# Sparse attention and a mixture of experts: row sends with mask products between them, and a routing without pieces on the shared port

## The chip, the cores and the metric

The kernel runs on one core of one Trainium2 chip. The time is the device time of one execution in microseconds (us). Three runs of the kernel before took 984.45, 992.74 and 991.97 us, a median of 991.97 us. The execution that the profiler recorded took 990.66 us; its span, from the first to the last recorded instruction, is 988.6 us.

The engines are TensorE (PE, with its weight loads as PEld), VectorE (DVE), ScalarE (ACT), GpSimd (POOL) and SyncE (SP, which issues DMAs). Each runs its own instructions in a fixed order.

## The reference

Two layers follow each other. The first is attention for 4 batches of 8 heads, 576 positions, 64 values per head, in which each query keeps only its 32 largest scores. The second is a layer of 8 experts over the 2304 rows of 512 values that attention gives; each row goes to the two experts with the largest noisy logits.

```python
scores = scale * np.matmul(q, k.transpose(0, 1, 3, 2))
kth = np.partition(scores, -top_k, axis=-1)[..., -top_k:-top_k + 1]   # top_k = 32
scores = np.where(scores >= kth, scores, -1000000000.0)
attn = np.exp(scores - max) / sum;  out = np.matmul(attn, v)
...
noisy_logits = x @ w_gate + np.log1p(np.exp(x @ w_noise)) * noise
top2_w = softmax of the two largest noisy logits of a row
h = np.maximum(x[mask] @ w1[e], 0.0)                                  # 512 -> 1024
out[mask] += top2_w[mask, k, None] * (h @ w2[e])                      # 1024 -> 512
```

## The kernel before

**Attention.** A tile is 128 queries of one head against its 576 keys; 36 tiles make a batch, 144 all four. For a tile PE computes the scores into two PSUM banks (L602, L606), ScalarE copies the first half to SBUF (L614), VectorE folds the halves to their maxima and minima (L636) and finds the 32nd largest value by rounds of "eight largest" (L649) and "replace these eight" (L654). In some tiles (the table `DROPS`, in tenths of a batch's tiles) one replacement is done by ScalarE and GpSimd instead: a sign (L660) and a product (L663). A small piece makes the exponential's bias (L670, on GpSimd or VectorE). A mask of what is below the 32nd value is made by ScalarE (L717, with its threshold from L713) or by VectorE (L679). The **mask product** (L727, nearly always on GpSimd) puts the mask on the scores, ScalarE takes the exponential (L675), PE transposes the tile (L750, L754), ScalarE copies it (L759, L763), and PE multiplies it with the values (L812 to L824). Rows are scaled by their sums (L870 to L882) and collected in `xr`. From batch 1 on keys and queries are split into a high and a low part (L537, L541, L544).

**Routing.** After a batch's 36 tiles its logits are ready. `route` computes the noise scale, the two largest logits, the gates and the slot of each row in its expert's list with small pieces on ScalarE, VectorE and GpSimd (L985 to L1062). Then GpSimd issues ten **row sends**, indirect DMAs that write each row of `xr` into its two experts' lists in DRAM (`scatter`, L1111, with a small memset before each, L1110). They are issued in a chain in which a send waits only until the one ahead has begun.

**Experts.** The lists are worked off in five groups: rows 0 to 127 of all 8 experts after batch 0, rows 128 to 255 of experts 4 to 7 after batch 1, and after batch 2 rows 256 to 383 of experts 4 to 7 and rows 128 to 383 of experts 0 to 3; the last group, 256 rows of all experts, comes after batch 3. SP loads the rows (L1205), PE transposes them (L1236) and multiplies. One-tile groups use plain float32 (L1301, L1328). The two groups with two tiles split each weight into a high half (ScalarE, L1182) and a low half (L1186, on GpSimd or VectorE) and take three products per pair (L1270 to L1272 up, L1336 to L1338 down). A **unit** is one such up and down step for 128 of an expert's 1024 hidden values; a group of four experts has 32 units, the last one 64. Results go out by indirect DMAs on GpSimd (L1356).

**The order.** All pieces are given to a planner (`Plan`, L93) with an engine, a planned duration, what they need, and a priority; it plays the engines' clocks forward and writes down the order in which each engine then runs its instructions. A piece with an `alt` can go to a second engine, and tables by batch (`BIAS`, `BELOW`, `NORM`, `OUTS`, `LOWS`) weigh the choice. `PACE` and `WHEN` set priorities of expert work, transposes and routing against attention. Until the first expert rows are there PE's idle times are filled with matmuls on a dummy tile (`filler`, L564). The planned durations are not times of the chip; they only move the order. The sends of batch b are added like this:

```python
scat.append(add("POOL", 1280, scatter(t, k), [x, g, AVN["tok", b]] + [(s, True) for s in scat[-1:]] + FILLS,
                move=750, lat=700))
```

## Time and profile before

| | |
|---|---|
| median of three runs | 991.97 us (984.45 to 992.74) |
| profiled execution | 990.66 us, span 988.6 us |
| PE busy | 926.3 us, 94% |
| VectorE busy | 683.0 us, 69% |
| ScalarE busy | 651.5 us, 66% |
| GpSimd busy | 650.5 us, 66% |
| row sends (L1111) | 40, 40.9 us |
| mask products on GpSimd (L727) | 141, 187.4 us |
| low weight halves on GpSimd (L1186) | 79, 194.6 us |

Busy time is an average over parts of the span with different limits, so it is read by stretches. A busy PE is not PE at its peak, since matmuls overlap and their ends are modelled. In the timeline an idle time stands in brackets with what ended it. A line such as L727 is the line of the kernel above.

### The profile page before, as it was taken

The page shows a single profiled execution, that of the slowest core. Times are in us where ns is not written, and L with a number is a line of the kernel's source. Part 1 is how long each engine was busy: PE and PEld are TensorE (multiplying, and loading weights), DVE is VectorE, ACT ScalarE, POOL GpSimd, SP SyncE. Part 2 cuts the span into 40 slices and gives each one's busy share as a digit, 9 for nine tenths or more (in the row PEclk, how much of TensorE's full clock was granted, in tenths as well). Part 3 has the DMA queues.
Part 4 walks back from the last instruction along what each step waited for, and adds up shares of the span by engine and source line. Part 5 has one row for each costly group of instructions (what it writes and reads, how often), then busy time and mean ns, then how long its engine had stood idle before and what let it go on. Part 6 is the DMA issues. An engine that isn't in the chain of part 4 may idle for free.

```text
span 988.6 us, 18573 instructions
## 1 busy us (share of the span) xinstructions
PE 926.3 (94%) x6229; PEld 711.0 (72%) x6246; DVE 683.0 (69%) x2191; ACT 651.5 (66%) x1502; POOL 650.5 (66%) x819
## 2 busy tenths in 40 slices
PE   9999999799999778999989999999898999999993
PEld 4555566477778567777767777778787999998992
DVE  7999989989999969999979992347644222222220
ACT  4888887388988467988737873356644555555550
POOL 4566576646755856566676662238878898888881
PEclk9999999999999989999999999999999999999997
DMA  9464521346687566665856787785658687777741
GB/s 288 161 208 151 174 71 45 110 124 192 189 235 190 209 194 175 189 204 185 227 190 207 229 264 244 260 266 202 171 160 272 213 253 224 226 228 235 214 107 25
DMA packets 122250, 190.61 MB, mean 193 GB/s; under 512 B 8224, under 2 KB 69664, under 8 KB 122144
## 3 DMA queue, kind: packets, MB, share of 16 engines
q1 hardware_dynamic: 113440, 169.10, 54.0%
q0 software_dynamic: 8704, 20.22, 9.4%
q8 instruction: 51, 0.84, 0.3%
q14 instruction: 55, 0.45, 0.2%
HBM read 153.02 MB, written 36.27 MB: 191 GB/s over the span
## 4 chain that ended last, share of the span: by engine, by line
PE 59%; DVE 17%; ACT 8%; POOL 6%; issue 4%; DMA 2%; another core or an unknown queue 1%; SPq 0%; POOLq 0%; DVEq 0%; ACTq 0%
PE hps L1301 6%; DVE t8s L649 6%; PE bk L1328 6%; PE bk L602 5%; DVE cat L654 4%; PE hps L564 4%; PE hps L1270 4%; PE hps L1272 4%; PE hps L1271 4%; PE pp L750 4%; PE bank L812 3%; DVE cat L636 3%; PE bk L606 3%; PE bk L1336 2%; PE bk L1337 2%
## 5 line engine op out<-in xcount | busy, mean ns | idle before, releaser
L649 DVE MAX8 t8s<-cat 128x8 f32<-128x288 f32 (+3 forms) x576 | 265.3, 489 | 4.7 <-POOL cat L663 2.4
L727 POOL TENSOR_TENSOR ss<-ss,mk 128x576 f32<-128x576 f32 x141 | 187.4, 1331 | 76.5 <-ACT mk L717 57.2
L1186 POOL TENSOR_TENSOR wl<-wr,wh 128x1024 fp32r<-128x1024 f32 x79 | 194.6, 2529 | 35.8 <-ACT wh L1182 29.5
L654 DVE MATCH_REPLACE8 cat<-t8s,cat 128x208 f32<-128x208 f32 (+2 forms) x415 | 162.7, 394 | 0.0
L636 DVE TENSOR_TENSOR cat<-bk,ss 128x288 f32<-128x288 f32 x288 | 126.3, 443 | 34.7 <-ACT ss L614 28.3
L675 ACT ACTIVATE ss<-ss,nb 128x576 f32<-128x576 f32 x144 | 112.6, 782 | 39.9 <-POOL ss L727 37.1
L614 ACT ACTIVATE ss<-bk 128x288 f32<-128x288 f32 x288 | 111.5, 416 | 39.6 <-PE bk L606 15.1
L1328 PE MATMUL bk<-wr,hh 128*128 128x512 f32 x256 | 127.8, 595 | 0.0
L1301 PE MATMUL hps<-xh,wr 128*128 128x128 f32 x1024 | 127.5, 279 | 0.0
L1301 PEld LDWEIGHTS hps<-xh,wr 128*128 128x128 f32 x1024 | 123.1, 195 | 5.2 <-issue 4.0
L1182 ACT ACTIVATE wh<-wr 128x1024 fp32r<-128x1024 f32 x96 | 99.8, 1055 | 34.8 <-PE bk L1338 17.1
L1280 DVE SCALAR_TENSOR_TENSOR hl<-hps,hh 128x256 fp32r<-128x256 f32 x96 | 40.3, 422 | 111.2 <-ACT hh L1276 109.5
L1270 PE MATMUL hps<-xh,wh 128*128 128x256 f32 x384 | 111.3, 290 | 0.2
L606 PE MATMUL bk<-hi 128*128 128x288 f32 x240 | 88.9, 380 | 24.1 <-ACT ss L614 12.6
L1272 PE MATMUL hps<-xh,wl 128*128 128x256 f32 x384 | 108.8, 283 | 0.4 <-POOL wl L1186 0.4
L1271 PE MATMUL hps<-xl,wh 128*128 128x256 f32 x384 | 108.6, 283 | 0.0
L717 ACT ACTIVATE mk<-ss,under 128x576 bf16<-128x576 f32 x118 | 91.2, 778 | 19.8 <-POOL under L713 11.2
L759 ACT ACTIVATE pt<-pp 128x512 f32<-128x512 f32 x144 | 86.8, 603 | 15.3 <-PE pp L750 14.3
L750 PE MATMUL pp<-ident,ss 128*128 128x128 f32 x576 | 90.2, 279 | 6.4 <-ACT pt L759 3.6
L750 PEld LDWEIGHTS pp<-ident,ss 128*128 128x128 f32 x576 | 66.4, 142 | 40.4 <-ACT pt L759 11.9
L1356 POOL DMA_INDIRECT out_dram<-yo,tok x40 | 65.1, 1627 | 38.1 <-ACT yo L1352 29.8
L564 PE MATMUL hps<-dummy 128*128 128x512 bf16 x283 | 80.0, 395 | 2.4 <-DVE dummy L458 0.9
(159 smaller groups left out, 1910.5 us busy)
## 6 DMA issues: line engine op xcount, KB each, us to landing
wr<-in_w_dram SPq DMA_DIRECT2D x224, 512.0 KB
raw<-in_qk_dram SPq DMA_DIRECT2D x48, 320.0 KB
xg<-xs SPq DMA_DIRECT2D x16, 528.0 KB
xs<-xg SPq DMA_DIRECT2D x12, 528.0 KB
vt<-in_v_dram SPq DMA_DIRECT2D x32, 192.0 KB
out_dram<-xs SPq DMA_DIRECT2D x1, 5120.0 KB
xs<-xg SPq DMA_DIRECT2D x16, 264.0 KB
hi<-in_qk_dram SPq DMA_DIRECT2D x8, 320.0 KB
```

The source lines that it names most:

```text
L564: nc.tensor.matmul(ps, C["dummy"].to_broadcast([128, 128]), C["dummy"].to_broadcast([128, 512]), start=True, stop=True)
L636: nc.vector.tensor_tensor(o, t["sp", 1], t["s"][:, :HS], op=op)
L649: return lambda: nc.vector.max(t["t8"][:, r], t["cat"] if r == 3 else t["cat"][:, slice(*TAKE[r])])
L654: nc.vector.match_replace(g, t["t8"][:, r], g, NEG)
L727: ENG[eng].tensor_tensor(t["s"], t["s"], t["mk"], op=OP.subtract)
L750: nc.tensor.transpose(pp[:, c], t["s"][:, k0 + c * 128:k0 + (c + 1) * 128], ident)
L1186: return lambda eng: ENG[eng].tensor_tensor(WS[m][1][:, i], W[m][:, i], WS[m][0][:, i].bitcast(F32), op=OP.subtract)
L1270: nc.tensor.matmul(ps[:, :NN], ah, xh, start=(c == 0), stop=False)
L1271: nc.tensor.matmul(ps[:, :NN], ah, xl, start=False, stop=False)
L1272: nc.tensor.matmul(ps[:, :NN], al, xh, start=False, stop=(c == 3))
L1301: nc.tensor.matmul(ps[:, f * 128:(f + 1) * 128], w[:, 0, a:a + 128], X["h", e][:, c, :128], start=(c == 0), stop=(c == 3))
L1328: nc.tensor.matmul(Y[e][0], HN["h", ff // 2][:, f * 128:(f + 1) * 128], W[4 * e + ff // 2][:, 1, f * 512:(f + 1) * 512], start=(ff == 0), ...
```

## The change

Sends get a `gap`: the planner does not start a send before 1500 or 1600 of its nanoseconds have passed since its end of the one ahead (`SGAP`; `SLOT` 1 means every send), and other pieces take the time. In the routing GpSimd makes ex + 1 once (`one_more`) for its own error term and for VectorE's reciprocal, where VectorE made it a second time with a tensor_scalar; the marker column of `odd` is made by a scalar_tensor_tensor with a constant tile `away`. Planned durations of routing, value products, sums and output sends, and the tables of choices and priorities, are set anew.

```diff
-BIAS = (500, 500, 500, 500)
-BELOW = (1100, -3300, 2200, 4100)
+BIAS = (2000, 500, 500, 500)
+BELOW = (1100, -3100, 2200, 4500)
...
-LOWN = 16
+LOWN = 13
...
-DROPS = (4, 0, 1, 0)
+DROPS = (4, 0, 2, 0)
...
-WHEN = (16, 13, -21, -20)
+SGAP, SLOT = (1500, 1600, 1600, 1500), (1, 1, 1, 1)
+
+WHEN = (16, 13, -21, -12)
...
-PACE = [(70, 54), (900, 40), (90, 13), (300, 13), (0, 0)]
+PACE = [(70, 54), (910, 40), (110, 23), (300, 18), (0, 0)]
...
+            if x.gap:
+
+                at = self.sent + x.gap
+                if at > t:
+                    heapq.heappush(wait[e], (at, x.n, x))
+                    continue
...
+            if x.gap is not None:
+                self.sent = t + x.dur
...
         def err():
 
-            G.tensor_scalar(new("q", [NT, 8]), st["ex"], 1.0, None, op0=OP.add)
-            G.tensor_scalar(st["q"], st["q"], 1.0, None, op0=OP.subtract)
+            G.tensor_scalar(new("q", [NT, 8]), st["u"], 1.0, None, op0=OP.subtract)
             G.tensor_tensor(st["q"], st["q"], st["ex"], op=OP.subtract)
 
+        def one_more():
+            G.tensor_scalar(new("u", [NT, 8]), st["ex"], 1.0, None, op0=OP.add)
+
         def part():
-            V.tensor_scalar(new("u", [NT, 8]), st["ex"], 1.0, None, op0=OP.add)
-            V.reciprocal(st["u"], st["u"])
+            V.reciprocal(new("ru", [NT, 8]), st["u"])
...
-            V.tensor_scalar(new("tm", [2, NT, 9])[:, :, :, 8], st["c1"][:, None, :].to_broadcast([128, 2, NT]), 2.0, float(E * STRIDE),
-                            op0=OP.not_equal, op1=OP.mult)
+            V.scalar_tensor_tensor(new("tm", [2, NT, 9])[:, :, :, 8], st["c1"][:, None, :].to_broadcast([128, 2, NT]), 2.0,
+                                   C["away"][:, None, :].to_broadcast([128, 2, NT]), op0=OP.not_equal, op1=OP.mult)
...
-                                move=750, lat=700))
+                                move=750, lat=700, gap=(SGAP[b] if len(scat) % SLOT[b] == 0 else 0) if scat else 0))
```

The order on GpSimd where batch 1's rows are sent; L1110 and L1111 are a send with its memset. Before, from the end of the gates (L1030) on (six more sends follow, then the mask product L727):

```order
L1030 TENSOR_TENSOR xr<-p 128x5x8
L544 TENSOR_TENSOR hi<-raw,hi 64x640
L1110 MEMSET spacer 1x1
L1111 DMA xg<-xr,si 40960x528
L1110 MEMSET spacer 1x1
L1111 DMA xg<-xr,si 40960x528
L1110 MEMSET spacer 1x1
L1111 DMA xg<-xr,si 40960x528
L1110 MEMSET spacer 1x1
L1111 DMA xg<-xr,si 40960x528
```

After, where the mask product is L739, a send L1125, the bias L682 and an output send L1370:

```order
L1124 MEMSET spacer 1x1
L1125 DMA xg<-xr,si 40960x528
L725 TENSOR_SCALAR under<-t8s 128x1 x2
L739 TENSOR_TENSOR ss<-ss,mk 128x576
L1124 MEMSET spacer 1x1
L1125 DMA xg<-xr,si 40960x528
L739 TENSOR_TENSOR ss<-ss,mk 128x576
L725 TENSOR_SCALAR under<-t8s 128x1
L1369 MEMSET spacer 1x1
L1370 DMA out_dram<-yo,tok 2560x512
L1124 MEMSET spacer 1x1
L1125 DMA xg<-xr,si 40960x528
```

Between the first and the last send of a batch there are now 6, 8 and 6 mask products in batches 0, 1 and 2, where there was none. In batch 3, after attention, low weight halves (L1200) and output sends stand between them:

```order
L1043 TENSOR_TENSOR xr<-p 128x5x8
L1124 MEMSET spacer 1x1
L1125 DMA xg<-xr,si 40960x528
L1200 TENSOR_TENSOR wl<-wr,wh 128x1024
L1124 MEMSET spacer 1x1
L1125 DMA xg<-xr,si 40960x528
L1369 MEMSET spacer 1x1
L1370 DMA out_dram<-yo,tok 2560x512
L1124 MEMSET spacer 1x1
L1125 DMA xg<-xr,si 40960x528
```

On PE, the last tile's transposes (L750 before) stood among the units of the first two-tile group (L1270 to L1272 and L1336 to L1338); 14 of its 32 units were ahead of them:

```order
L1270 MATMUL hps<-xh,wh 128x256
L1271 MATMUL hps<-xl,wh 128x256
L1272 MATMUL hps<-xh,wl 128x256
L750 MATMUL pp<-ident,ss 128x128 x4
L754 MATMUL bank<-ident,ss 128x128
L1336 MATMUL bk<-wh,hh 128x512
L1337 MATMUL bk<-wl,hh 128x512
```

After, the same transposes (L762) stand among the last steps of the one-tile groups (L1315, L1342), and the first step of the first two-tile unit (L1284) follows:

```order
L1315 MATMUL hps<-xh,wr 128x128 x8
L1250 MATMUL hps<-ident,xs 128x128 x2
L762 MATMUL pp<-ident,ss 128x128 x4
L766 MATMUL bank<-ident,ss 128x128
L1250 MATMUL hps<-ident,xs 128x128 x2
L1342 MATMUL bk<-wr,hh 128x512
```

All 32 units now stand behind attention's last tile. At the front of PE's order 51 tiles' transposes stand ahead of the first expert transpose (45 before), with 314 filler matmuls (300 before). VectorE makes 19 of the 96 low halves (17 before), all after attention; 4 of batch 0's bias pieces (19 before); and 21 of the copies of L849 (27 before).

## Rows read from the trace of the kernel before

**Rows 1.** The page: busy time by engine; busy tenths in 40 slices.

```profile
PE 926.3 (94%) x6229; PEld 711.0 (72%) x6246; DVE 683.0 (69%) x2191; ACT 651.5 (66%) x1502; POOL 650.5 (66%) x819
...
PE   9999999799999778999989999999898999999993
...
DVE  7999989989999969999979992347644222222220
```

**Rows 2.** Windows: length, busy PE, PEld, DVE, ACT, POOL; clock, DMA share, GB/s.

```profile
180.00:200.00 20.00, 15.88 (x78) 9.22 (x77) 15.67 (x56) 7.43 (x17) 12.56 (x23) 0.91 0.36 123
...
340.00:360.00 20.00, 12.48 (x63) 9.21 (x62) 12.96 (x45) 6.82 (x18) 10.23 (x19) 0.83 0.51 175
500.00:520.00 20.00, 15.26 (x92) 11.39 (x89) 13.49 (x52) 6.64 (x16) 15.19 (x31) 0.93 0.64 211
...
600.00:728.00 128.00, 123.52 (x839) 99.42 (x838) 63.03 (x174) 67.23 (x153) 67.14 (x65) 1.00 0.69 220
```

**Rows 3.** Timeline of GpSimd: start, length, what, idle before; batches 0 and 1.

```profile
188.94 0.92 POOL L1111 DMA_INDIRECT xg<-xr,si  x1 [0.23 <-issue]
...
334.13 1.13 POOL L1111 DMA_INDIRECT xg<-xr,si  x1 [0.17 <-POOL spacer L1110]
...
346.06 0.92 POOL L1111 DMA_INDIRECT xg<-xr,si  x1 [0.24 <-issue]
347.04 1.27 POOL L727 TENSOR_TENSOR ss<-ss,mk 128x576 f32<-128x576 f32 x1
```

**Rows 4.** Timeline of VectorE, its idle times behind the sends of batches 0, 1, 2.

```profile
201.37 0.21 DVE L874 RECIPROCAL rs<-sums 128x9 f32<-128x9 f32 x1 [4.96 <-POOL sums L870]
...
350.51 0.46 DVE L636 TENSOR_TENSOR cat<-bk,ss 128x288 f32<-128x288 f32 x1 [2.58 <-ACT ss L614]
...
355.04 0.46 DVE L636 TENSOR_TENSOR cat<-bk,ss 128x288 f32<-128x288 f32 x1 [3.06 <-ACT ss L614]
...
365.98 0.22 DVE L874 RECIPROCAL rs<-sums 128x9 f32<-128x9 f32 x1 [2.25 <-POOL sums L870]
...
519.14 0.46 DVE L636 TENSOR_TENSOR cat<-bk,ss 128x288 f32<-128x288 f32 x1 [6.21 <-issue]
```

**Rows 5.** Timeline of PE: first expert matmul, a stall, last transposes, two units.

```profile
206.23 1.95 PE L1301 MATMUL hps<-xh,wr 128*128 128x128 f32 x16
...
350.23 0.61 PE L606 MATMUL bk<-hi 128*128 128x288 f32 x1 [7.52 <-ACT ss L614]
...
714.71 0.60 PE L750 MATMUL pp<-ident,ss 128*128 128x128 f32 x4
...
820.90 0.36 PE L1270 MATMUL hps<-xh,wh 128*128 128x256 f32 x1
...
823.95 0.36 PE L1270 MATMUL hps<-xh,wh 128*128 128x256 f32 x1
```

**Rows 6.** Waits of PE: us in total, times, longest.

```profile
PE hps L1272 <- POOL wl L1186: 0.4, 1, 0.4
```

**Rows 7.** Groups by line: count, busy us, mean ns, idle before.

```profile
L564 PE MATMUL hps<-dummy 128*128 128x512 bf16 x283 | 80.0, 395 | 2.4 <-DVE dummy L458 0.9 <-issue 0.9
...
L670 DVE TENSOR_SCALAR nb<-t8s 128x1 f32<-128x1 f32 x63 | 12.7, 202 | 0.6
...
L849 DVE COPY xr<-bank 128x256 f32<-128x256 f32 (+1 forms) x27 | 9.6, 355 | 26.9 <-PE bank L841 24.5 <-PE bank L754 0.9 <-ACT pt L925 0.9
```

**Rows 8.** Single lines: ns least, median, most; first and last start.

```profile
L999 DVE TENSOR_SCALAR u<-ex x4: 333/1116/1330, 163.1 to 728.2; 128x40 f32<-128x40 f32 x4
...
L1054 DVE TENSOR_SCALAR tm<-c x4: 1023/1406/2134, 170.0 to 735.7; 128x10 f32<-128x10 f32 x4
...
L1047 DVE TENSOR_TENSOR tm<-rank,oh x4: 244/274/1222, 174.7 to 738.2; 128x80 f32<-128x80 f32 x4
...
L1186 POOL TENSOR_TENSOR wl<-wr,wh x79: 2372/2415/3012, 660.2 to 960.9; 128x1024 fp32r<-128x1024 f32 x79
...
L1186 DVE TENSOR_TENSOR wl<-wr,wh x17: 1204/1224/2015, 663.1 to 950.6; 128x1024 fp32r<-128x1024 f32 x17
```

More of the change, by code (lines that the diff above doesn't have):

```diff
@@ L38 @@
 WEIGHS = (700, 2400, 2100, 3400)
-BIAS = (500, 500, 500, 500)
-BELOW = (1100, -3300, 2200, 4100)
+BIAS = (2000, 500, 500, 500)
+BELOW = (1100, -3100, 2200, 4500)
 LOWK = (2300, 1900, 500, 2600)
-OUTS = (300, 300, 300, 100)
-NORM = (3000, 400, -100, -200)
-LOWS = (2100, 1600, 2300)
-LOWN = 16
+OUTS = (300, -100, 300, 300)
+NORM = (3000, 400, -100, -1700)
+LOWS = (2100, 1600, 2700)
+LOWN = 13
 def spread(i, tenths):
@@ L84 @@
           (3, 384, 2, range(8))]
-PACE = [(70, 54), (900, 40), (90, 13), (300, 13), (0, 0)]
+PACE = [(70, 54), (910, 40), (110, 23), (300, 18), (0, 0)]
 class Node:
-    __slots__ = ("eng", "dur", "fn", "deps", "users", "prio", "left", "ready", "lat", "start", "n", "share", "move", "bank", "alt", "ready2", "shy", "lock")
+    __slots__ = ("eng", "dur", "fn", "deps", "users", "prio", "left", "ready", "lat", "start", "n", "share", "move", "bank", "alt", "ready2", "shy", "lock", "gap")
 class Plan:
@@ L105, in __init__, with add @@
         self.nodes, self.rings, self.prio, self.pauses = [], {}, 0, []
-    def add(self, eng, dur, fn, deps=(), prio=None, lat=0, share=1.0, move=0, bank=False, alt=None, lock=False):
+    def add(self, eng, dur, fn, deps=(), prio=None, lat=0, share=1.0, move=0, bank=False, alt=None, lock=False, gap=None):
         x = Node()
@@ L112, in add @@
         x.users, x.start, x.n, x.bank, x.alt = [], None, len(self.nodes), bank, alt
-        x.shy, x.lock = None, lock
+        x.shy, x.lock, x.gap = None, lock, gap
         self.nodes.append(x)
@@ L472, in sparse_attention_moe @@
     C["spacer"] = cp.tile([1, 1], F32, name="spacer")
+    C["away"] = cp.tile([128, NT], F32, name="away")
+    nc.vector.memset(C["away"], float(E * STRIDE))
     C["iota8"] = cp.tile([128, 8], F32, name="iota8")
@@ L825, in few @@
                                      stop=(c == 4), skip_group_check=True)
-        av = add("PE", 1200 if rest else 2350, few if rest else values, [x for m in pairs for x in PAIR[m]], share=0.5, bank=True)
+        av = add("PE", 735 if rest else 2315, few if rest else values, [x for m in pairs for x in PAIR[m]], share=0.5, bank=True)
         for m in pairs:
@@ L882, in norm @@
             ENG[eng].tensor_tensor(o, o, NN["r"][:64, 8:10, None].to_broadcast([64, 2, D]), op=OP.mult)
-        p1 = add("POOL", 170, plus, [T[i]["mid"][0] for i in range(j // 9 * 9, j // 9 * 9 + 9)])
-        r = add("DVE", 190, recip, [p1])
+        p1 = add("POOL", 345, plus, [T[i]["mid"][0] for i in range(j // 9 * 9, j // 9 * 9 + 9)])
+        r = add("DVE", 418, recip, [p1])
         br = pl.take("rs", 2, r)
@@ L1091, in route @@
         x1 = add("ACT", 220, ln, [x0])
-        x2 = add("POOL", 560, err, [x0])
-        pa = add("DVE", 330, part, [x0])
-        x2 = add("POOL", 760, noised, [x1, x2, pa, AVN["ax", b]])
+        x2 = add("POOL", 425, one_more, [x0])
+        pa = add("DVE", 325, part, [x2])
+        x2 = add("POOL", 765, err, [x2])
+        x2 = add("POOL", 1270, noised, [x1, x2, pa, AVN["ax", b]])
         x3 = add("DVE", 1200, top, [x2])
-        g = a2 = add("POOL", 320, apart2, [x3])
+        g = a2 = add("POOL", 440, apart2, [x3])
         g = add("ACT", 120, exp2, [g])
         g = add("DVE", 290, whole, [g])
-        g = add("POOL", 640, gates, [g, AVN["xr", b]])
+        g = add("POOL", 950, gates, [g, AVN["xr", b]])
         pm = add("PE", 880, mm, [x3], share=0.2, bank=True)
         pp = pl.take("ps_l", 1, pm)
-        od = add("DVE", 330, odd, [a2])
-        x = add("DVE", 690, slots, [pm, od, prev["cntn"] if prev else None], bank=True)
+        od = add("DVE", 340, odd, [a2])
+        x = add("DVE", 1000, slots, [pm, od, prev["cntn"] if prev else None], bank=True)
         pl.give(pp, x)
@@ L1363, in down @@
                     po = pl.take("yo", 2, y)
-                    z = add("POOL", 1280, st, [y], move=750, lat=700)
+                    z = add("POOL", 1850, st, [y], move=750, lat=700)
                     pl.give(po, z)
```

4 lines of the change are left out of this document (2 added, 2 removed).

## The prediction

> **What bounds the kernel now.** I read the page first. PE is busy for 94% of the span, no other engine for more than 69%, but the slices of the span show two halves: VectorE is at 9 tenths almost everywhere until the 24th slice (it ends at about 593 us) and then falls to 2 to 7 tenths and stays at 2 in the end, while PE stays at 9 [rows 1]. So attention runs at VectorE's pace where PE has little to do (batch 0: there are no expert rows yet and PE is kept going by filler matmuls), at the pace of both engines in batches 1 and 2, and at PE's pace from then on: between 600 and 728 us PE is busy for 123.5 of 128 us and VectorE for 63.0 [rows 2].
>
> The second look goes to the slices that break this pattern, 180 to 200, 340 to 360 and 500 to 520 us: PE drops to 15.9, 12.5 and 15.3 of 20 us, VectorE to 15.7, 13.0 and 13.5 [rows 2]. These are the places where GpSimd sends the rows of a batch. GpSimd's timeline shows batch 1's ten sends from 334.13 to 346.98 us, 1.3 us apart and with nothing but each send's own small memset between them; the first mask product stands behind the last one, at 347.04 [rows 3]. A mask product of 1.27 us feeds each tile's exponential, so for 13 us no tile can go on, and PE, ScalarE and VectorE run dry as their buffers fill.
>
> The third view, each engine's timeline behind the bursts, gives the size: VectorE stood idle for 4.96 us behind batch 0's sends, for 2.58, 3.06 and 2.25 behind batch 1's and for 6.21 behind batch 2's, 19.1 us in all [rows 4]; PE stood still for 7.52 us at once behind batch 1's [rows 5]. Batch 3's sends come after attention, where nothing but expert weights waits for GpSimd.
>
> **The change, part by part.** The times are set against the profiled execution, 990.66 us (span 988.6 us); the median of the three runs is 991.97, 1.3 us above it.
>
> *Sends apart.* The order after the change puts 6, 8 and 6 mask products between the first and the last send of batches 0, 1 and 2. Ten sends of 1.3 us and 6 to 8 products of 1.27 us [rows 3] make 20.5 to 23 us of GpSimd's time, with the small steps and key halves among them some 25 us, where 13 us stood before. In them 6 to 8 tiles move on, and none did. The gain is bounded by 0 (every stall comes back elsewhere) and 19.1 us (all of it goes). I take two thirds, **-12.7 us**: a product can still be late by one send (1.3 us), and the products wait in GpSimd's order for ScalarE's masks. What is late next is the last send, by about 12 us in each batch. In batch 0 the first expert matmul came 16.4 us after the last send's end (189.86, from 188.94 and 0.92 [rows 3]; 206.23 [rows 5]), so it comes later too; the order shows what PE does instead, 51 tiles' transposes ahead of the first expert transpose where 45 stood. That is attention work moved forward, not waiting. In batches 1 and 2 the rows sent are used only by the next groups, which stand 10 to 25 tiles later in PE's order.
>
> *Fillers.* PE's order holds 314 filler matmuls, 300 before. At 80.0 us for the 283 recorded [rows 7], 0.28 us each, 14 more are **+4.0 us** (0 if they only fill time in which PE would wait; I keep the 4).
>
> *Clock.* The granted clock was 0.91, 0.83 and 0.93 in the three slices [rows 2], against 1.00 from 600 to 728 us: 1.8, 3.4 and 1.4 us lost if PE had been busy throughout, 4.6 us at its busy shares of 0.79, 0.62 and 0.76. It was lowest in the slice where PE had stood still for 7.52 us. Part of that loss lies inside the stalls already counted, so I take **-2 us** (0 to -4.6).
>
> *Routing.* The +1 moves from VectorE to GpSimd (L999, median 1.12 us, least 0.33 [rows 8]), and the tensor_scalar of L1054 (median 1.41 us for ten columns [rows 8]) becomes a scalar_tensor_tensor that reads a second tile. The new form is not in the trace. Its nearest row is L1047, a two-tile operation of 80 columns: least 0.24, median 0.27, most 1.22 us [rows 8]. So each routing gives VectorE 1.3 to 2.3 us. A rule speaks against this edit: by the Trainium skill, SBUF — State Buffer, section "Who interferes with whom", a VectorE instruction with two inputs in SBUF still contends with a GpSimd instruction that reads SBUF, and whoever comes second is blocked for the whole of the other. By that rule the new form would often cost the 1.22 us and this edit would give the 1.3 us; the median of L1047 sides with 2.3 where GpSimd is not reading. GpSimd's own chain gets no shorter, since VectorE's reciprocal now waits for GpSimd's +1.
>
> *Constants.* They change only the order and who does a piece. In batch 0, 15 of the bias pieces go from VectorE to GpSimd (19 left it, now 4): 15 x 0.20 = 3.0 us of VectorE [rows 7]. GpSimd was 66% busy [rows 1] and hides them. Six copies of 0.36 us [rows 7] go from VectorE to ScalarE, four side drops more go to ScalarE and GpSimd. Batch 0, where VectorE alone sets the pace, gains 3.0 + 1.3 to 2.3 us, and I take 4.5; batches 1 and 2, where PE is as full as VectorE, gain 0 to 2.3 each and the copies 0 to 2.1, and I take 1.5: together **-6 us** (0 to -12).
>
> *The end of attention.* In PE's order 14 of the 32 units of the first two-tile group stood ahead of attention's last transposes; now none does. A unit is 3.05 us here (820.90 to 823.95 [rows 5]), so 43 us of expert work moves behind attention, and attention itself comes that much earlier; on a full PE this is a swap at no cost. Its cover is the supply of low weight halves. Around batch 3's sends GpSimd now has 4 halves, 10 sends and 3 output sends in one stretch, and VectorE makes more of the halves. PE waited 0.4 us for a half in the whole run [rows 6]. Between nothing and 20 us I take the end that this row is nearest to, **+2 us**.
>
> Sum: -12.7 + 4.0 - 2 - 6 + 2 = -14.7, so 990.66 - 14.7 = **976 us**.
>
> **The rivals.** *All of it comes back.* Every stall goes (-19.1), the clock stays up (-4.6), VectorE's pieces count in full (-12), and only the fillers are paid (+4): 959 us. For it: PE is the bound from 600 us on and idle nowhere else for long. Against it: a GpSimd in strict order between two engines that wait for it has hardly a stretch without small waits. Chance 0.13.
>
> *The stall is spread out, not removed.* With a send ahead of nearly every product, each tile is late by up to 1.3 us in VectorE's pace, and a send stands behind a product that waits for ScalarE. One third of the stall comes back (-6.4), 3 us of VectorE's pieces, nothing of the clock, +4 for fillers, +4 at the end of attention: 989 us. For it: GpSimd was busy 15.2 of the 20 us from 500 to 520 [rows 2], and some 25 us of its work must now fit into about 28 us beside all four engines' waits. Against it: VectorE and PE had free time of 5 to 8 us in each burst that nothing could use. Chance 0.22.
>
> *Slower: halves blocked at the port.* After attention VectorE must make 19 halves beside GpSimd's own. In the trace a half took VectorE 1.20 us at least and 2.02 at most, GpSimd 2.42 [rows 8]; the 17 that VectorE made were mostly not held up. If each of the 19 is held for one GpSimd half, PE is late by 19 x 2.42 = 46 us, and at half of that by 23: 976 + 23 = 999 us. It decides against the forecast from about 15 us on, six of the 19 held in full. The same section of the Trainium skill (SBUF — State Buffer) has this as its rule: two SBUF inputs against a GpSimd reader, the second fully blocked. By that rule the time would be the 999; the medians (1.22 against a least of 1.20) say that the order keeps them apart so far. Chance 0.09.
>
> **How the numbers follow.** The forecast, 966 to 985 us, has chance 0.56. One per cent, 9.9 us, is about what a measurement of this kernel can tell from no change; the three runs shown lie between 984 and 993. Faster by over 1% (under 982): 0.53 of the forecast and the 0.13 of full recovery, 0.66. Within 1%: 0.03 of the forecast, 0.20 of the spread-out stall, 0.03 of the blocked halves, 0.26. Slower by over 1%: 0.06 of the blocked halves and 0.02 of the spread-out stall, 0.08. The range from 961 to 992 leaves out about half of the full recovery (0.06), some of the spread-out stall (0.06) and most of the blocked halves (0.08).
>
> **What would show it.** In the changed profile: 6 to 8 mask products between the first and last send of batches 0 to 2, and VectorE's idle rows behind them at 6 us together, not 19; no slice of PE under 15 of 20 us until the end; first expert matmul some 5 to 10 us later than 206, with about 297 recorded fillers; the last tile's transposes near 645 to 670 us, where they stood at 714.71 [rows 5] (714.7 less the 43 us of expert work and a gain of some 13 us); PE's waits for halves under 3 us. The prediction is wrong if VectorE's idle time comes back as many waits of about 1 us between the sends, if PE waits on ScalarE in the same places, or if PE's idle time after attention passes 15 us.

## The result, and the profile after

The changed kernel takes **956.79 us** (median of 4 runs, 954.62 to 957.88) against 991.62 us for the kernel before beside it (4 runs, 984.45 to 992.74): a ratio of 0.9651, interval 0.9603 to 0.9700. The forecast was 976 us with a range down to 961; the gain is 34.8 us where the steps added up to 14.7. The profiled execution of the change took 957.39 us, its span is 955.5 us.

Later runs, on five chips, put a second number beside it. On four of them the kernel before takes 973.4 to 974.4 us, on one 992.2; the change takes 956.3 us on one of the four, a ratio of 0.9823 (0.9796 to 0.9849). So about half of the first difference belongs to what the kernel before does on some chips only, and about half to the change on any of them. Each of these chips was used in one set of runs, and the chip of the first set is not on record, so a chip and its occasion are not told apart here. The experiments below take the two halves apart.

The page of the changed kernel, for [rows 1]: busy time by engine, and the slices of PE, of VectorE and of the granted clock.

```profile
PE 916.4 (96%) x6239; PEld 706.7 (74%) x6260; DVE 665.6 (70%) x2161; ACT 655.9 (69%) x1516; POOL 655.7 (69%) x840
...
PE   9999999999999899899999999999989999999992
...
DVE  7999989998999999899998893773543222222220
...
PEclk9999999999999999999999999999999999999996
```

PE's idle time in the span fell from 62.3 us (988.6 less 926.3 [rows 1]) to 39.1 us, and its busy time by 9.9 us; the two make the span's 33.1 us. Before, PE ran 20.5 us of the span at 1.2 GHz in five places before its end; after, none (the last slice alone is at 6 tenths in the row).

The windows that answer to [rows 2], columns as there:

```profile
180.00:200.00 20.00, 18.70 (x149) 12.35 (x152) 18.32 (x73) 14.23 (x36) 15.40 (x24) 1.00 0.39 130
...
340.00:360.00 20.00, 20.00 (x162) 14.78 (x161) 19.70 (x69) 15.40 (x42) 16.81 (x30) 1.00 0.89 283
500.00:520.00 20.00, 20.00 (x178) 15.87 (x175) 19.38 (x65) 14.46 (x42) 14.75 (x25) 1.00 0.91 281
600.00:728.00 128.00, 124.49 (x859) 104.59 (x859) 69.43 (x195) 73.58 (x154) 84.99 (x94) 1.00 0.74 237
```

The three holes are gone: PE is busy for 18.7, 20.0 and 20.0 of 20 us at full clock, VectorE for 18.3 to 19.7.

GpSimd's timeline, batch 0's first sends and its last one, for [rows 3]:

```profile
177.93 1.24 POOL L1125 DMA_INDIRECT xg<-xr,si  x1 [0.19 <-POOL spacer L1124]
...
180.17 1.28 POOL L739 TENSOR_TENSOR ss<-ss,mk 128x576 f32<-128x576 f32 x1
181.39 0.09 POOL L1124 MEMSET spacer<- 1x1 f32 x1
181.64 1.06 POOL L1125 DMA_INDIRECT xg<-xr,si  x1 [0.16 <-issue]
...
206.40 0.92 POOL L1125 DMA_INDIRECT xg<-xr,si  x1 [0.18 <-issue]
```

The ten sends now take from 177.93 to 207.32 us with six products among them. VectorE's idle times over 1 us at and behind the sends of batches 0, 1 and 2, for [rows 4]:

```profile
196.58 0.28 DVE L894 TENSOR_TENSOR xr<-xr,rs 64x128 f32<-64x128 f32 x1 [1.07 <-ACT xr L859]
...
335.88 0.46 DVE L648 TENSOR_TENSOR cat<-bk,ss 128x288 f32<-128x288 f32 x1 [1.95 <-ACT ss L626]
...
523.50 0.82 DVE L648 TENSOR_TENSOR cat<-bk,ss 128x288 f32<-128x288 f32 x2 [1.83 <-ACT ss L626]
...
531.02 0.82 DVE L648 TENSOR_TENSOR cat<-bk,ss 128x288 f32<-128x288 f32 x2 [3.02 <-ACT ss L626]
```

These are 7.9 us together where the five rows of [rows 4] had 19.1. PE's first expert matmul and the last transposes of attention, for [rows 5], then PE's longest waits and that for a weight half, for [rows 6]:

```profile
217.12 2.06 PE L1315 MATMUL hps<-xh,wr 128*128 128x128 f32 x17
...
641.47 0.60 PE L762 MATMUL pp<-ident,ss 128*128 128x128 f32 x4
```

```profile
PE pp L762 <- ACT ss L687: 2.7, 5, 1.1
PE hps L1315 <- DMA wr<-in_w_dram: 2.4, 3, 1.1
PE hps L1284 <- DVE hl L1294: 2.4, 2, 1.2
...
PE hps L1286 <- POOL wl L1200: 0.4, 1, 0.4
```

Attention ends 73 us earlier (641.47, before 714.71 [rows 5]), more than the 45 to 70 us forecast; between the later profiles `before_again` and `after_again` it is 58 us (698.80 to 640.70). The first expert matmul comes 10.9 us later (217.12, before 206.23 [rows 5]), a little more than the 5 to 10 us forecast, and PE still waits 0.4 us for a half. The filler group for [rows 7], and the single lines for [rows 8] (least, median, most):

```profile
L576 PE MATMUL hps<-dummy 128*128 128x512 bf16 x293 | 81.4, 388 | 2.0 <-DVE dummy L468 0.9 <-issue 0.5
```

```profile
L1013 DVE RECIPROCAL ru<-u x4: 391/392/396, 165.8 to 663.3; 128x40 f32<-128x40 f32 x4
...
L1067 DVE SCALAR_TENSOR_TENSOR tm<-c,away x4: 177/1432/1905, 173.2 to 668.5; 128x10 f32<-128x10 f32 x4
...
L1200 DVE TENSOR_TENSOR wl<-wr,wh x19: 1215/1215/1708, 676.3 to 916.9; 128x1024 fp32r<-128x1024 f32 x19
```

### The profile page after: what moved, and what is told of

It reads as the page before. It is cut to its first block, busy times and chain, and to the rows that moved or that the text cites. A ratio compares the mean times of both kernels' runs of the same rounds, so it can differ in the third digit from the quotient of the medians.

```text
span 955.5 us, 18621 instructions
## 1 busy us (share of the span) xinstructions
PE 916.4 (96%) x6239; PEld 706.7 (74%) x6260; DVE 665.6 (70%) x2161; ACT 655.9 (69%) x1516; POOL 655.7 (69%) x840
## 4 chain that ended last, share of the span: by engine, by line
PE 76%; DMA 5%; POOL 5%; ACT 5%; DVE 4%; issue 3%; SPq 1%; POOLq 0%; DVEq 0%; ACTq 0%
PE bk L1342 9%; PE hps L1315 8%; PE pp L762 6%; PE bank L824 5%; PE hps L576 5%; PE bk L618 5%; PE hps L1284 5%; PE hps L1286 4%; PE hps L1285 4%; PE bk L614 4%; PE bk L1350 3%; PE bk L1351 3%; PE bk L1352 3%; DMA wr<-in_w_dram 2%; PE hps L1250 2%
## 5 line engine op out<-in xcount | busy, mean ns | idle before, releaser
L739 POOL TENSOR_TENSOR ss<-ss,mk 128x576 f32<-128x576 f32 x143 | 186.0, 1304 | 76.8 <-ACT mk L729 60.5
L1200 POOL TENSOR_TENSOR wl<-wr,wh 128x1024 fp32r<-128x1024 f32 x77 | 188.1, 2479 | 33.7 <-ACT wh L1196 33.5
L666 DVE MATCH_REPLACE8 cat<-t8s,cat 128x240 f32<-128x240 f32 (+2 forms) x411 | 161.3, 395 | 0.0
L1315 PEld LDWEIGHTS hps<-xh,wr 128*128 128x128 f32 x1024 | 120.7, 192 | 11.4 <-issue 5.0
L1315 PE MATMUL hps<-xh,wr 128*128 128x128 f32 x1024 | 125.2, 276 | 3.2 <-DMA wr<-in_w_dram 2.4
L1342 PE MATMUL bk<-wr,hh 128*128 128x512 f32 x256 | 127.2, 594 | 0.0
L626 ACT ACTIVATE ss<-bk 128x288 f32<-128x288 f32 x288 | 109.1, 412 | 22.9 <-PE bk L614 12.3
L1284 PE MATMUL hps<-xh,wh 128*128 128x256 f32 x384 | 111.1, 289 | 2.4 <-DVE hl L1294 2.4
L729 ACT ACTIVATE mk<-ss,under 128x576 bf16<-128x576 f32 x118 | 91.5, 777 | 18.4 <-POOL under L725 13.7
L618 PE MATMUL bk<-hi 128*128 128x288 f32 x240 | 91.1, 389 | 2.9 <-POOL hi L556 1.3
L762 PE MATMUL pp<-ident,ss 128*128 128x128 f32 x576 | 89.5, 278 | 3.1 <-ACT ss L687 2.7
L762 PEld LDWEIGHTS pp<-ident,ss 128*128 128x128 f32 x576 | 66.2, 142 | 35.4 <-issue 10.2
L1370 POOL DMA_INDIRECT out_dram<-yo,tok x40 | 65.9, 1647 | 26.9 <-ACT yo L1366 16.5
L576 PE MATMUL hps<-dummy 128*128 128x512 bf16 x293 | 81.4, 388 | 2.0 <-DVE dummy L468 0.9
```

Of the source, the lines that this page charges most:

```text
L576: nc.tensor.matmul(ps, C["dummy"].to_broadcast([128, 128]), C["dummy"].to_broadcast([128, 512]), start=True, stop=True)
L618: nc.tensor.matmul(sp, lhs(n), rhs, start=(k == 0), stop=(k == 2 * len(heads) - 1))
L666: nc.vector.match_replace(g, t["t8"][:, r], g, NEG)
L739: ENG[eng].tensor_tensor(t["s"], t["s"], t["mk"], op=OP.subtract)
L762: nc.tensor.transpose(pp[:, c], t["s"][:, k0 + c * 128:k0 + (c + 1) * 128], ident)
L1200: return lambda eng: ENG[eng].tensor_tensor(WS[m][1][:, i], W[m][:, i], WS[m][0][:, i].bitcast(F32), op=OP.subtract)
```

## The experiments

The theories at first: that the sends set apart are the gain (S), or that the constants are (C). Once both had fallen, theory F: the parts fit each other, and the time hangs on the one order that the planner makes from all the numbers. Each ratio is to the kernel before on the same chip, with its interval.

### One part, or all but one

The change has three parts: sends apart (the `gap`), the routing edit (pieces and planned durations of the routing), and the constants (tables and other planned durations).

Sends apart alone (`gap_only`), in the kernel before, with the planner's lines for `gap`:

```diff
+SGAP, SLOT = (1500, 1600, 1600, 1500), (1, 1, 1, 1)
...
-                                move=750, lat=700))
+                                move=750, lat=700, gap=(SGAP[b] if len(scat) % SLOT[b] == 0 else 0) if scat else 0))
```

> The kernel before with nothing but the gap between the sends. Theory S: 960 to 968 us, no stretch at 1.2 GHz before the end. Theory C: 980 us or more.

Measured: 980.59 us, ratio **1.0069** (1.0044 to 1.0094).

All but the sends apart (`no_gap`), in the changed kernel:

```diff
-                                move=750, lat=700, gap=(SGAP[b] if len(scat) % SLOT[b] == 0 else 0) if scat else 0))
+                                move=750, lat=700, gap=None))
```

> The changed kernel with the gap between the sends taken away (routing and constants as changed): the sends stand back to back again. Theory S (the sends set apart are the gain): 980 to 990 us, VectorE again idle 5 us or more behind batches 0 to 2, and stretches at 1.2 GHz again. Theory C (the constants are the gain, above all the new paces that put attention ahead of the first two-tile group): 960 to 968 us, the stalls there but covered.

Measured: 971.67 us, **0.9987** (0.9972 to 1.0003).

Constants alone (`const_only`), in the kernel before: the tables from `BIAS` to `PACE`, and six planned durations outside the routing:

```diff
-PACE = [(70, 54), (900, 40), (90, 13), (300, 13), (0, 0)]
+PACE = [(70, 54), (910, 40), (110, 23), (300, 18), (0, 0)]
...
-        av = add("PE", 1200 if rest else 2350, few if rest else values, [x for m in pairs for x in PAIR[m]], share=0.5, bank=True)
+        av = add("PE", 735 if rest else 2315, few if rest else values, [x for m in pairs for x in PAIR[m]], share=0.5, bank=True)
...
```

> The kernel before with the new constants alone (tables, paces, planned durations outside the routing). Theory S: 983 to 995 us. Theory C: 960 to 970 us.

Measured: 966.32 us, **0.9933** (0.9900 to 0.9966).

All but the routing edit (`no_route`), in the changed kernel; the pieces go back with their durations:

```diff
-        x2 = add("POOL", 425, one_more, [x0])
-        pa = add("DVE", 325, part, [x2])
-        x2 = add("POOL", 765, err, [x2])
-        x2 = add("POOL", 1270, noised, [x1, x2, pa, AVN["ax", b]])
+        x2 = add("POOL", 560, err, [x0])
+        pa = add("DVE", 330, part, [x0])
+        x2 = add("POOL", 760, noised, [x1, x2, pa, AVN["ax", b]])
...
```

> The changed kernel with the routing of before (pieces and planned durations). Both theories: 955 to 962 us. If the routing's pieces were worth the 1.3 to 2.3 us of VectorE per batch that the prediction gave them and VectorE set the pace, 961 to 966 us; the changed trace shows the new marker piece at a median of 1.43 us against 1.41 us before, so I expect the lower end.

Measured: 976.33 us, **1.0028** (1.0009 to 1.0046).

Routing edit alone (`route_only`), the same lines the other way round in the kernel before:

> Only the new routing (its pieces and its planned durations) in the kernel before. Theory F: no gain, 968 to 980 us. Rival (the routing's planned durations, nearer to the measured ones, are the gain by themselves): 960 us or less.

Measured: 972.65 us, **0.9990** (0.9973 to 1.0006).

All but the constants (`no_const`), the lines of `const_only` put back in the changed kernel:

> Sends apart and the new routing, with the constants of the kernel before. Theory F: without the constants that were set for it the order fits no better than with the sends alone, 970 to 982 us. Rival (routing and sends are what pays, constants are only trim): within 4 us of the whole change, 955 to 961 us.

Measured: 978.29 us, **1.0043** (1.0022 to 1.0065).

The whole change again (`after_again`), no line other:

> The whole change, timed on the chip on which the kernel before takes 973.4 us and not 991.6. Theory F (the gain is one of fit: sends set apart, the new routing and the constants pay only together, since the order of the work is planned from all of them): the change takes about as long as in its first runs, 955 to 959 us, a ratio to before of 0.981 to 0.985, and clearly below the best of its parts so far (constants alone, 966). Theory B (the kernel before is what varies: in its first runs its stalls happened to be long, and the change was worth far less all along): the change comes out at 963 us or more here, a ratio over 0.99, no better than the constants alone.

Measured: 956.25 us, **0.9823** (0.9796 to 0.9849).

The three parts alone give +0.69%, -0.10% and -0.67%, nothing in sum; any two of them give +0.28%, +0.43% and -0.13%; all three give -1.77%. No part is the gain. The sends apart cost 0.5 to 1.0% in three settings (alone, beside the constants, beside the routing: 0.9990 to 1.0043) and gain 1.6% beside both (0.9987 to 0.9823). Theory F, stated behind the first four of these runs, held for the three others.

### Why the kernel before took 991 us

The kernel before, unchanged, profiled on a chip where it takes 974 us (`before_again`).

> The kernel before, with a profile on this chip, where it takes 973 us and not 991. Theory B: its span is about 970 us, and what is gone against the first profile are the stalls behind the bursts of sends: VectorE's 19.1 us there come down to under 8, and the half-clock stretches of TensorE (five before 800 us in the first profile) to two or fewer. Rival: the bursts stall it as they did (15 to 20 us behind them), and the 18 us are missing all over the span, a level of this chip, in which case the time of the change moves by the same share, to about 940 us.

Measured: 975.37 us, span 973.4, 15.2 us less than the first profile of the same program. ScalarE's timeline shows where. First that of the first profile, in and behind the bursts of batches 0, 1 and 2 (start, length, what, idle before and its releaser):

```profile
185.92 0.19 ACT L675 ACTIVATION_READ_ACCUMULATOR ss<-ss,nb 128x1 f32 x1
191.78 0.71 ACT L614 ACTIVATE ss<-bk 128x288 f32<-128x288 f32 x2 [5.67 <-remote]
...
348.74 0.38 ACT L1306 ACTIVATE hh<-hps 128x256 f32<-128x256 f32 x1 [7.66 <-remote]
...
518.70 0.41 ACT L614 ACTIVATE ss<-bk 128x288 f32<-128x288 f32 x1 [2.37 <-remote]
```

Then the same place of the same program on the other chip:

```profile
186.66 0.19 ACT L675 ACTIVATION_READ_ACCUMULATOR ss<-ss,nb 128x1 f32 x1
188.45 0.71 ACT L614 ACTIVATE ss<-bk 128x288 f32<-128x288 f32 x2 [1.60 <-PE bk L606]
```

The instruction after L675 copies scores that PE has just made. On the second chip it starts at 188.45 us, as soon as PE is done (188.41). On the first PE is done at 187.66 us and the copy starts at 191.78, 4.1 us later; "remote" says that the profile names no instruction as its releaser. The trace's records of the semaphores do: the one that this copy waits for is raised by PE's matmuls on the same core. Matmuls that end at 187.40, 187.67 and 188.34 us have their updates on record only at 191.71, 191.75 and 191.81, and the copy starts with them. Behind batch 1's sends matmuls that end at 340.70, 341.85 and 342.71 us have theirs at 348.72, 348.78 and 348.82, up to 8.0 us late, and L1306 starts at 348.74. So it is PE's signal that is late, and ScalarE waits for it. The end of a matmul is modelled, but on the second chip each of PE's 1044 ends that raise this semaphore has an update within 0.1 us of it. In the first profile 35 of 1043 have none so near (late, or not recorded), 26 of them between a batch's first send and 3 us behind its last. The sends themselves are alike, ten at 1.3 us each from 177.10 to 189.86 there and from 177.85 to 190.60 here. The windows show what hangs on it, first of the first profile, then of this one (from 180, 380 and 660 us):

```profile
180.00:380.00 200.00, 181.46 (x1328) 138.22 (x1327) 180.46 (x628) 145.75 (x368) 124.54 (x192) 0.97 0.64 188
380.00:590.00 210.00, 197.49 (x1439) 152.16 (x1441) 198.05 (x641) 160.78 (x409) 138.32 (x202) 0.99 0.69 205
...
660.00:800.00 140.00, 130.42 (x861) 113.50 (x860) 71.47 (x188) 81.62 (x154) 116.06 (x105) 0.99 0.68 212
```

```profile
180.00:380.00 200.00, 190.71 (x1394) 144.89 (x1394) 190.14 (x657) 156.24 (x393) 130.93 (x200) 0.98 0.67 197
380.00:590.00 210.00, 202.25 (x1480) 156.83 (x1481) 190.92 (x627) 158.44 (x406) 138.42 (x203) 0.99 0.73 216
...
660.00:800.00 140.00, 130.88 (x872) 115.21 (x871) 65.09 (x164) 79.26 (x146) 118.11 (x107) 0.99 0.67 204
```

PE is busy 9.3 and 4.8 us more in the two stretches that hold the bursts of batches 0 to 2, and not in the third, which holds batch 3's sends after attention. Tile by tile (by the starts of ScalarE's copies of the transposed scores, L759, counted in their order), from the 39th to the 43rd takes 33.6 us in the first profile and 28.3 in the second, from the 74th to the 78th 37.1 and 28.2, from the 114th to the 118th 32.0 and 27.0: 19.2 us in the three bursts, and some of it made up behind them. So the stall of [rows 4] and [rows 5] is real on that chip, and not a price of the burst on every chip: on the second, VectorE's longest idle times behind the same bursts are 0.5, 1.5 and 1.6 us.

```profile
196.86 0.22 DVE L874 RECIPROCAL rs<-sums 128x9 f32<-128x9 f32 x1 [0.48 <-POOL sums L870]
...
365.99 0.46 DVE L636 TENSOR_TENSOR cat<-bk,ss 128x288 f32<-128x288 f32 x1 [1.53 <-ACT ss L614]
...
514.03 0.52 DVE L679 TENSOR_SCALAR mk<-ss,t8s 128x576 bf16<-128x576 f32 x1 [1.60 <-POOL ss L727]
```

The rival of a slower chip all over the span falls. The expectation of two half-clock stretches or fewer was wrong: four are left before the end, 13.7 us.

### The fit of the order

One planned duration nudged by 4 ns in the changed kernel, with nothing else changed (`nudge_after`):

```diff
-            k = add("DVE", 71, below, [d], alt=("POOL", 306, BELOW[b]))
+            k = add("DVE", 75, below, [d], alt=("POOL", 306, BELOW[b]))
```

> The changed kernel with one planned duration nudged: the small VectorE comparison ahead of each mask is planned at 75 ns in place of 71. Nothing that runs is other, only the order that is planned from the numbers. Theory F (the gain of the constants and of the whole is one of fit: this order happens to leave little idle): the nudge alone costs 5 to 25 us, 962 to 981. Rival M (the gain is a mechanism: sends apart and a routing that is planned near its measured durations keep TensorE fed whatever the exact order): within 4 us of the change, 953 to 960.

Measured: 969.65 us, **0.9935** (0.9910 to 0.9961). The pieces are the same; their order differs, and with it who does some of them (GpSimd makes 105 of the bias pieces of L682 where it made 93). 13 of the 18 us are gone. The chip is not the reason: with the change's own order it takes 955.5 us there (`compare_back`, below).

A further theory, G, was set against F from here on: the sends apart shift the times of all orders down, and the first nudge was a bad draw. The same line's GpSimd duration 306 to 312 (`nudge_below_after`):

```diff
-            k = add("DVE", 71, below, [d], alt=("POOL", 306, BELOW[b]))
+            k = add("DVE", 71, below, [d], alt=("POOL", 312, BELOW[b]))
```

> The changed kernel, the small comparison planned at 312 ns in place of 306 where GpSimd takes it (one of the constants of the change, 179 before). Theory F: 960 to 981 us. Theory G: 953 to 961.

Measured: 965.94 us, **0.9917** (0.9894 to 0.9941).

The mask planned at 670 ns in place of 667 (`nudge_mask_after`); its chip is the one where the kernel before takes 992.18 us:

```diff
-            mk = add("ACT", 667, over_it, [k])
+            mk = add("ACT", 670, over_it, [k])
```

> The changed kernel, the mask on ScalarE planned at 670 ns in place of 667. Theory F (one fitting order out of a spread): 962 to 981 us, as the first nudge (969.7). Theory G (the sends apart shift the whole spread down, the first nudge was a bad draw): 953 to 961.

Measured: 968.21 us, **0.9759** (0.9719 to 0.9799).

The same two nudges of the kernel before, on that chip too (`nudge_before` 71 to 75, `nudge_mask_before` 667 to 670):

> The kernel before, the small comparison planned at 75 ns in place of 71. Theory F: the kernel before was fitted to its own numbers as well, so a nudge makes it slower, 975 to 995 us. Theory G: no such thing, it moves by under 4 us either way, 970 to 978.

> The kernel before, the mask on ScalarE planned at 670 ns in place of 667. Theory F: 975 to 995 us. Theory G: 970 to 978.

Measured: 994.38 us, **1.0039** (1.0008 to 1.0070), and 993.23 us, **1.0031** (1.0001 to 1.0062). The absolute times of the expectation are of the other chips; by ratio both moved by under 4 us, as theory G says. On this chip, where all three times hold the stall, the kernel before was no lucky order.

And of the change with its sends in one burst, the first on that chip, the second on a chip where the kernel before takes 973.35 us (`nudge_burst` 71 to 75, `nudge_mask_burst` 667 to 670):

> The change with its sends in one burst (971.7 us), the small comparison planned at 75 ns in place of 71. Theory F: within the spread of the nudged change, 962 to 985 us. Theory G: no faster than without the nudge, 970 us or more, and slower than both nudged versions of the change.

> The change with its sends in one burst, the mask on ScalarE planned at 670 ns in place of 667. Theory F: 962 to 985 us, overlapping the nudged versions of the change. Theory G: 970 us or more, slower than every nudged version of the change.

Measured: 993.74 us, **1.0017** (0.9993 to 1.0041), and 985.21 us, **1.0134** (1.0108 to 1.0161).

With the constants and the routing of the change, the four orders with the sends apart take 955.4 to 969.7 us on chips without the stall (the fourth is `old_durations`, below), the two with one burst 971.7 and 985.2; on the chip with the stall it is 968.2 against 993.7. That fits theory G, but so few orders, 2 us apart at the nearest, are a sign and no proof; and G's 953 to 961 us failed for both nudged orders it was put to (968.2 and 965.9), where theory F's ranges held. The order as it stands is among the good draws: on chips without the stall the nudged ones take 965.9 and 969.7 us, the change 956.3.

The chip of `nudge_burst` shows the stall again. Its rows there in `nudge_burst`, at the bursts of batches 0, 1, 2 and 3:

```profile
192.22 0.71 ACT L626 ACTIVATE ss<-bk 128x288 f32<-128x288 f32 x2 [7.40 <-remote]
...
352.63 0.38 ACT L1320 ACTIVATE hh<-hps 128x256 f32<-128x256 f32 x1 [6.85 <-remote]
...
516.39 0.38 ACT L1320 ACTIVATE hh<-hps 128x256 f32<-128x256 f32 x1 [5.25 <-remote]
...
716.80 0.38 ACT L1290 ACTIVATE hh<-hps 128x256 fp32r<-128x256 f32 x1 [5.84 <-remote]
```

In `nudge_before`, at the same instruction as in the first profile; then in `nudge_mask_before`, where the profile puts the same wait of 7.66 us behind batch 1's sends down to PE:

```profile
191.34 0.71 ACT L614 ACTIVATE ss<-bk 128x288 f32<-128x288 f32 x2 [5.64 <-remote]
```

```profile
348.62 0.38 ACT L1306 ACTIVATE hh<-hps 128x256 f32<-128x256 f32 x1 [7.66 <-PE bk L606]
```

In `nudge_mask_after`, the waits of ScalarE that are greatest in total; no "remote" is in the list:

```profile
ACT hh L1290 <- PE hps L1286: 63.7, 40, 2.6
ACT ss L687 <- POOL ss L739: 33.9, 32, 5.6
```

On one chip and in one set of runs, then, three kernels with bursts have the stall and the one with the sends apart has not. That kernel takes 968.2 us there, within the 965.9 to 969.7 of its sister orders elsewhere. Late signals it has too: PE's ends without an update within 0.1 us are 31 to 37 in the three with bursts, 19 in `nudge_mask_after` and 25 in the first profile of the change, against 0 to 2 in each of the fourteen profiles of the other four chips. But with the sends apart the late updates that can be matched to an end come at most 1.5 us behind it (in the change 195.55 for an end at 194.03), not 8.0.

### Durations or pieces of the routing

The changed kernel planned with the old durations of the routing (`old_durations`):

```diff
-        x2 = add("POOL", 425, one_more, [x0])
-        pa = add("DVE", 325, part, [x2])
-        x2 = add("POOL", 765, err, [x2])
-        x2 = add("POOL", 1270, noised, [x1, x2, pa, AVN["ax", b]])
+        x2 = add("POOL", 190, one_more, [x0])
+        pa = add("DVE", 165, part, [x2])
+        x2 = add("POOL", 370, err, [x2])
+        x2 = add("POOL", 760, noised, [x1, x2, pa, AVN["ax", b]])
...
```

> The changed kernel with the routing pieces as changed but planned with the durations of the kernel before (one more 190, part 165, err 370, noised 760, gates as after 320 and 640, odd 330, slots 690 ns). Rival D (the planned durations, near the measured ones, are what the routing edit gives): as slow as the change without its routing edit, 974 to 979 us. Rival P (the pieces moved off VectorE are it): within 4 us of the change, 953 to 960. Theory F: in between or worse, anywhere from 962 to 981, since any other order than the fitted one loses.

Measured: 955.36 us, **0.9800** (0.9777 to 0.9823). Theory F's 962 to 981 us did not come true here: another order, as good as the change's.

The old pieces planned with durations near the new ones (`old_pieces`), as a change to `no_route`:

```diff
-        x2 = add("POOL", 560, err, [x0])
-        pa = add("DVE", 330, part, [x0])
-        x2 = add("POOL", 760, noised, [x1, x2, pa, AVN["ax", b]])
+        x2 = add("POOL", 1190, err, [x0])
+        pa = add("DVE", 650, part, [x0])
+        x2 = add("POOL", 1270, noised, [x1, x2, pa, AVN["ax", b]])
...
```

> The changed kernel with the routing pieces of the kernel before (the first piece back on VectorE, the comparison without the second SBUF operand), planned with durations near the new ones (err 1190, part 650, noised 1270, 440, 950, 340, 1000 ns). Rival D: within 4 us of the change, 953 to 960. Rival P: like the change without the routing edit, 974 to 979. Theory F: 962 to 981 whichever it is.

Measured: 983.79 us, **1.0102** (1.0076 to 1.0127), above all three ranges. Rival D falls. With the sends apart and the new constants, both orders with the old pieces (976.3 and 983.8 us) are slower than all four with the new ones on chips without the stall (955.4 to 969.7), which speaks for the pieces; but with orders that a 4 ns nudge moves by 13 us, two against four are a sign and no proof, and what the pieces would free is not shown.

One of the pieces can be tried without moving anything (`compare_back`), since the order stays the same row for row:

```diff
-            V.scalar_tensor_tensor(new("tm", [2, NT, 9])[:, :, :, 8], st["c1"][:, None, :].to_broadcast([128, 2, NT]), 2.0,
-                                   C["away"][:, None, :].to_broadcast([128, 2, NT]), op0=OP.not_equal, op1=OP.mult)
+            V.tensor_scalar(new("tm", [2, NT, 9])[:, :, :, 8], st["c1"][:, None, :].to_broadcast([128, 2, NT]), 2.0, float(E * STRIDE),
+                            op0=OP.not_equal, op1=OP.mult)
```

> The changed kernel with one instruction put back: the comparison of the routing reads one SBUF operand and a scalar, as before, in place of two SBUF operands; the order is the changed one, row for row. My prediction priced the edit at 1.3 us saved on each of 3 batches' path where a page's rule would give nothing. By the rule and the changed trace (1.43 us median against 1.41) nothing is lost: 955 to 958 us, ratio to the change within 0.002. Rival: the second operand is what costs, and the median falls to about 0.35 us with 1 to 3 us off the time, 953 to 955.

Measured: 955.47 us, **0.9805** (0.9784 to 0.9826), where the change has 0.9823. The line, to be set beside that of the changed kernel above:

```profile
L1067 DVE TENSOR_SCALAR tm<-c x4: 178/1432/1906, 173.7 to 670.3; 128x10 f32<-128x10 f32 x4
```

178/1432/1906 ns against 177/1432/1905: the edit of this instruction does nothing in this order.

## Why the prediction was wrong, step by step

The direction and the place were right: the three holes of [rows 2] closed, 6 products stand between batch 0's sends, attention ends earlier, and the halves are not late. The size failed, in two steps above all. Beside the stall and its clock the sum had 0 us in all (+4.0, -6 and +2); on chips without the stall the change is worth 17 to 18.

**The step that failed: *Constants*, with *Routing*, -6 us (0 to -12), and *The end of attention*, +2.** They were priced as pieces of an engine's time, one by one, and added to the sends apart. The runs show that they don't add: alone the parts are worth about +6.7, -1.0 and -6.5 us on chips without the stall (their ratios by 974), together -17.2. What these constants set is the order on all engines at once and who does each piece, and 4 ns in one of them is worth 13 us. Between `before_again` and `after_again` PE's idle time fell from 47.6 to 34.8 us and its busy time from 925.8 to 919.7. Their pages:

```profile
PE 925.8 (95%) x6246; PEld 709.9 (73%) x6246; DVE 681.4 (70%) x2191; ACT 651.1 (67%) x1502; POOL 650.1 (67%) x819
```

```profile
PE 919.7 (96%) x6260; PEld 707.6 (74%) x6260; DVE 665.1 (70%) x2161; ACT 656.2 (69%) x1516; POOL 656.3 (69%) x840
```

Nearly half of that idle time, 6.0 of 12.8 us, went from the stretch that I priced at +2. In `after_again`, and then, for 660 to 800 us alone, in `const_only` and `no_gap`:

```profile
180.00:380.00 200.00, 194.29 (x1440) 147.01 (x1440) 187.43 (x659) 161.08 (x405) 137.55 (x211) 0.99 0.63 190
...
660.00:800.00 140.00, 136.85 (x901) 122.95 (x901) 53.39 (x118) 78.99 (x133) 117.84 (x99) 1.00 0.78 240
```

```profile
660.00:800.00 140.00, 134.25 (x876) 119.81 (x875) 49.44 (x113) 74.56 (x126) 116.25 (x99) 1.00 0.78 236
```

```profile
660.00:800.00 140.00, 133.12 (x875) 119.26 (x874) 49.14 (x114) 75.57 (x127) 116.47 (x101) 1.00 0.80 247
```

From 660 to 800 us PE is busy for 136.9 us in place of 130.9, from 180 to 380 us for 194.3 in place of 190.7. Before, attention's last tiles lay in that late stretch (up to 699 us here, 715 in the first profile) among the two-tile groups; now it holds expert work beside batch 3's routing and sends alone. I saw that 43 us of expert work moved behind attention and called it a swap at no cost. PE is busy 6.0 us more here, 6.4 between the first two profiles (136.86 against 130.42). The swap by itself does not give that much: in `const_only` and `no_gap` attention also ends early (last transposes at 643.00 and 650.99 us), and PE is busy 3.4 and 2.2 us more than in `before_again`. What the rest hangs on is not shown.

***Sends apart*, -12.7 us (0 to -19.1): right in kind on the chip of the first runs, too small, and misread.** There the three bursts cost 19.2 us by the tiles and 15.2 of the span, nearly all of the bound where I took two thirds. But I had read "no tile can go on for 13 us" as the cause. On chips without the stall the same 13 us of sends leave VectorE idle for 0.5 to 1.6 us at a time, and the sends set apart alone cost 0.69%. The row that would have told was on hand: [rows 4] name ScalarE as the releaser of two of five waits and [rows 5] of PE's 7.52 us, and I passed over ScalarE's own rows, where "remote" stands. What the burst holds up on that chip is PE's signals (up to 8.0 us late), and not the tiles' mask products alone.

***Clock*, -2 us (0 to -4.6): too small.** I took three slices. The first profile has 20.5 us at 1.2 GHz in five places before the end, worth up to 10.2 us where PE was busy; the change has none. Between `before_again` (13.7 us) and `after_again` (3.4 us) the same gives up to 5.1, about the 6.1 us by which PE's busy time fell.

***Fillers*, +4.0 us: about right.** Where all of them are on record, 300 take 81.9 us (`before_again`) and 314 take 84.9 (`after_again`), 3.0 more. The 80.0 us [rows 7] and 81.4 of the first two profiles are of 283 and 293 recorded.

***Routing*, the port.** The Trainium skill, SBUF — State Buffer, section "Who interferes with whom", has the rule that a VectorE instruction with two SBUF inputs contends with GpSimd's reads. The new form's time fits it, 1.43 us median against 1.41 before [rows 8]; but the old form with one input takes as long in the same order (`compare_back`), so no run here shows that the second input is what waits. The form that I hoped to make cheap gained nothing. Its use against the halves did not come true: VectorE made 19 of them at a median of 1.22 us, most 1.71, and PE waited 0.4 us; the order keeps them apart.

**The rivals.** "All of it comes back" (959 us, 0.13) was nearest, within 2.2 us, though its sum has 19.1 us of stall that other chips don't have and too little for the order. "The stall is spread out" has the times of the sends apart alone or with one other part, 1.0028 to 1.0069, but its mechanism is not shown: alone they leave PE's idle time at 47.0 us, where `before_again` has 47.6. That the forecast's 976 is 0.985 of the profiled 990.66 and the ratio on other chips 0.982 is chance: the largest term of the sum has no place there.

**Open.** What holds PE's signals up; why some chips, or some occasions, have it; what in an order feeds PE well, and whether the sends apart shift all orders beside both other parts; whether the old pieces of the routing lose by themselves; which single constants make the order fit.

## What to carry to other kernels

Before a stall is priced, follow its chain to the first event that is late, in the semaphores' records where the profile names no releaser, and look whether the same program has it on a second chip: half of this gain was a stall that four of five later chips don't show. Where a planner sets the order, nudge one of its numbers by a few ns in both versions before crediting an edit; here that spread is 13 us, more than any part of the change alone. Parts of such a change are not to be priced one by one and added: three parts worth nothing in sum were worth 17 us together.

## What the hardware showed unasked

While GpSimd issues a burst of ten indirect sends (1.3 us each), PE's semaphore updates come late on some chips and not on others. In two of six sets of runs the four profiled kernels with bursts let ScalarE wait for up to 7.7 us at them (first profile 5.67, 7.66 and 2.37; `nudge_burst` 7.40, 6.85, 5.25 and 5.84), the updates stand up to 8.0 us behind the matmuls, and the kernels took 991 to 994 us. In the other four sets the five profiled kernels with bursts show no such wait, and each has at most one update that is not within 0.1 us of its end; on one of these chips no kernel with bursts was profiled, and the time of the kernel before, 974.1 us, speaks for it. With the sends apart the updates are late in the two first-named sets as well, by up to 1.5 us, and the time is that of the other chips: 956.8 against 956.3 us for the change.
